# Two PSUM banks that serve sums and filler alike, two open value segments, filled strips, a split root and new exp prices in a two-layer transformer kernel

## The chip, the cores and the metric

The kernel runs on one core of one Trainium2 chip. The metric is device time in microseconds. TensorE is called PE in the profile, VectorE DVE, ScalarE ACT, GpSimdE POOL, SyncE SP; PEld is TensorE's loading of weights.

## The reference

Two identical layers over x (2048 rows of 512): attention with 32 heads of 16 columns, then a dense block with 1792 hidden columns, each behind a layer norm and added to x.

```python
def _layernorm(x, axis=-1, eps=1e-5):
    m = jnp.mean(x, axis=axis, keepdims=True)
    v = jnp.var(x, axis=axis, keepdims=True)
    return (x - m) / jnp.sqrt(v + eps)
...
        scores = jnp.einsum("bhqd,bhkd->bhqk", q, k) * (Dh ** -0.5)
        p = _softmax(scores, axis=-1)
        o = jnp.einsum("bhqk,bhkd->bhqd", p, v)
...
        h = jnp.einsum("bsd,df->bsf", x, w1)
        h = jnp.maximum(h, zero)
        return jnp.einsum("bsf,fd->bsd", h, w2)
...
    x = x + _A_ref(_layernorm(x, axis=-1), A_wqkv, A_wo)
    x = x + _B_ref(_layernorm(x, axis=-1), B_w1, B_w2)
    x = x + _A_ref(_layernorm(x, axis=-1), A_wqkv, A_wo)
    x = x + _B_ref(_layernorm(x, axis=-1), B_w1, B_w2)
```

Everything comes in and goes out as bf16.

## The kernel before, in words

**The slots.** Scores are computed transposed, 128 keys by up to 512 queries of one head: a unit. The loop at L1566 walks all units of both layers, three to a slot (W = 3). In a slot, three score matmuls (L1714), each on 32 rows of the array, write three PSUM banks of ps_s; there are two such sets, used in turn. Then one exp on ScalarE (L1727) reads them and writes bf16 into one of five buffers e. The exp is either wide (all three units) or narrow (two units). In a narrow slot VectorE takes the third unit: its first step (L1299) turns the scores into int16 numbers in a buffer lin, and when two such blocks are there (a pair), GpSimd makes two shifted copies, up and down (L1354). The three together stand for the exp when each is multiplied with the values. There are six lin, three up and four down buffers. A slot is made narrow only if the conditions at L1590 to L1619 hold; one of them, lin_free, asks that the lin buffer six pairs back has been read by its value matmuls and copied by GpSimd.

**The value matmuls.** pv (L1171) multiplies an e, lin, up or down block with the values of one head, into 32 of the 128 partitions of the sums. Four heads fill the four strips of a round (v_round, L1213); the four matmuls of a round run side by side. A segment is one set of four heads, every second of eight, over a range of key blocks. Its sums collect in the bank ps_o. When no matmul of a segment remains, finish_segment (L1026) has VectorE copy the sums out (L1060, L1035 or L1058), and the next segment starts in ps_o after that copy. Only the current segment's blocks are looked at (v_ready with segs[seg_at[0]]).

**The filler.** All other matrix work (q, k, v, output projection, both dense matmuls, transposes of the normed rows) is cut into groups whose pieces stand in `urgent`, `work` and `cur`. A piece is a round of four matmuls on 32 columns each (L564). A group's sums collect in ps_f, and VectorE takes them out (for instance L874, L745, L781, L835, L914) before the next group starts there. Only in the very first slots, while `two[0]` holds, does filler use both banks.

**The planner.** The order on every engine is made when the program is built. Python code keeps a clock per engine (now_pe, now_dve, now_pool, exp_end) with prices: 216 ns for a round, 105 for a switch between kinds of matmul, 612 for an evacuation, and for an exp

```python
        exp_end[no] = begin + 1280.0 * place[m] / (W * QS) + 63.3
```

(L1735; place[m] is 1024 or 1536). For each slot it computes `limit`, the time until which TensorE may do other work without making the exp late (L1689), and fills that time with filler and value rounds (L1691 to L1695): first all filler that is owed, then values in rounds of at least three strips, then filler, or values first when four exps are pending. `owed` grows by `pace` per slot, the filler left over the slots left (L1673). If five exps are pending, force_v (L1259) makes value rounds at once. Where spare time is left, score matmuls are repeated.

**VectorE's order.** run_dve (L468) takes the evacuations of sums and the first steps (`musts`) ahead of filler evacuations, those ahead of tasks. A task is one entry however many instructions it has. The inverse root of a layer norm is one task (L673, ln_root at L616): per chunk of four row blocks four aggregations, two instructions for a first guess, four for a cubic step and three for a Newton step. It is priced RSTD = 1600 ns and is put at the head of the queue (place=0). Behind it come the normed rows (L636), and behind those the transposes, for some chunks by DMA on SyncE (L683).

**The tail.** After the loop the last values, projection, norm and dense block of the last 128 rows run by a written order (L1768 on).

## Time and profile before

| what | us |
|---|---|
| median of 3 runs (1453.84 to 1458.4) | 1454.89 |
| profiled execution | 1457.04 |
| its span, first to last instruction | 1455.3 |
| busy in it: ACT | 1388.2 |
| busy in it: PE | 1367.2 |
| busy in it: DVE | 1137.0 |
| busy in it: POOL | 711.3 |

A group's row names line, engine, operation, output and inputs with their shapes and the count; behind the first bar stand busy time in us and the mean length of one instruction in ns, behind the second the engine's idle time just before these instructions and what ended it. A row of the timeline begins with start and length in us, and merges neighbours of one kind. A row of the windows has the stretch, its length, each engine's busy time and count, TensorE's granted clock, the share of DMA time and GB/s. A row of waits names who waited for whom: us in total, times, the longest.

### The profile page before, as it was taken

How to read it: one execution, taken by the hardware profiler on the slowest of the kernel's cores; microseconds unless marked ns; L12 is line 12 of the kernel's file. 1: busy time of each engine (PE TensorE's matmuls, PEld its weight loads, DVE VectorE, ACT ScalarE, POOL GpSimd, SP SyncE). 2: the span in 40 equal slices, each digit the busy share in tenths (PEclk: the TensorE clock that was granted, in tenths of full speed). 3: DMA queues.
4: the chain of work that ended last, by engine and by line, in shares of the span. 5: the costliest groups of instructions: out<-in, count | busy, mean ns of one | idle time of the engine just before them, and what ended most of it. 6: DMA issues, size and time to landing. Idle time of an engine off the chain costs nothing.

```text
span 1455.3 us, 49098 instructions
## 1 busy us (share of the span) xinstructions
PE 1367.2 (94%) x20895; PEld 497.9 (34%) x20898; DVE 1137.0 (78%) x2078; ACT 1388.2 (95%) x1392; POOL 711.3 (49%) x1203
## 2 busy tenths in 40 slices
PE   6899889999999999999899999989999999999997
PEld 2322222222232222222222222223234444455665
DVE  5777668877887888887698777788888787877773
ACT  4999999999999999999999998999999999999994
POOL 3125555655545555565346453444544555555430
PEclk8999999999899999999999999999999999999999
DMA  5300000210102110121101100000110111132121
GB/s 131 96 5 17 21 21 2 46 39 17 24 8 47 28 31 10 29 49 25 23 2 31 34 5 2 6 18 17 42 42 16 43 37 25 30 83 66 26 49 31
DMA packets 135036, 46.41 MB, mean 32 GB/s; under 512 B 119680, under 2 KB 132032, under 8 KB 134816
## 3 DMA queue, kind: packets, MB, share of 16 engines
q1 hardware_dynamic: 127760, 37.14, 10.9%
q0 software_dynamic: 5568, 5.15, 1.9%
q8 instruction: 163, 2.67, 0.8%
q10 hardware_dynamic: 1488, 0.98, 0.2%
q14 instruction: 57, 0.47, 0.1%
HBM read 24.38 MB, written 2.10 MB: 18 GB/s over the span
## 4 chain that ended last, share of the span: by engine, by line
ACT 50%; PE 35%; DVE 12%; issue 3%; POOL 0%; DMA 0%; DVEq 0%; another core or an unknown queue 0%; ACTq 0%; POOLq 0%
ACT e L1727 50%; PE ps_s L1714 12%; PE ps_o L1175 11%; PE ps_f L564 10%; DVE lin L1299 5%; DVE stats L600 1%; PE ps_s L1801 1%; DVE vaug L781 1%; DVE ht L874 1%; PE ps_f L645 1%; DVE xn L636 0%; PE ps_f L557 0%; DVE ya L611 0%; DVE x L914 0%; DVE u L1060 0%
## 5 line engine op out<-in xcount | busy, mean ns | idle before, releaser
L1727 ACT ACTIVATE e<-ps_s 128x1024 bf16<-128x1024 f32 (+1 forms) x1366 | 1377.3, 1148 | 30.3 <-PE ps_s L1714 25.4
L1299 DVE TENSOR_SCALAR lin<-ps_s 128x512 int16<-128x512 f32 x1106 | 743.8, 686 | 179.8 <-PE ps_s L1714 124.9
L1354 POOL INT64_ADD up<-lin x553 | 340.0, 619 | 587.4 <-PE ps_o L1175 305.0
L1714 PE MATMUL ps_s<-q,ktp 32*128 32x512 bf16 (+2 forms) x5971 | 574.2, 328 | 45.2 <-ACT e L1727 27.6
L1354 POOL INT64_ADD down<-lin x553 | 342.2, 621 | 106.6 <-DVE lin L1299 50.4
L1175 PE MATMUL ps_o<-e,vaug 128*32 128x512 bf16 (+2 forms) x4124 | 365.2, 330 | 8.0 <-DVE r L1060 2.8
L1714 PEld LDWEIGHTS <-ktp 32*128 32x128 bf16 x5971 | 169.6, 91 | 513.5 <-issue 500.9
L1175 PEld LDWEIGHTS <-vaug 128*32 128x32 bf16 x7256 | 169.2, 95 | 228.7 <-issue 203.3
L1175 PE MATMUL ps_o<-up,vaug 128*32 128x512 bf16 (+2 forms) x1508 | 177.8, 324 | 0.0
L1175 PE MATMUL ps_o<-lin,vaug 128*32 128x512 bf16 (+2 forms) x1508 | 169.6, 324 | 1.6 <-DVE u L1060 1.0
L1175 PE MATMUL ps_o<-down,vscaled 128*32 128x512 bf16 (+2 forms) x1392 | 170.8, 326 | 0.0
L564 PE MATMUL ps_f<-xnT,w 128*32 128x512 bf16 (+1 forms) x1792 | 124.2, 356 | 4.6 <-DVE ht L874 2.1
L564 PE MATMUL ps_f<-w,ht 128*32 128x512 bf16 x1680 | 127.0, 382 | 1.3 <-DVE ht L874 0.5
L564 PE MATMUL ps_f<-xnT,wkq 128*32 128x512 bf16 (+2 forms) x1376 | 97.6, 357 | 3.9 <-DVE vaug L781 1.5
L874 DVE TENSOR_SCALAR ht<-ps_f 128x512 bf16<-128x512 f32 x105 | 71.7, 683 | 18.8 <-PE ps_f L564 16.9
L1175 PEld LDWEIGHTS <-vscaled 128*32 128x32 bf16 x1392 | 58.3, 96 | 20.6 <-issue 8.9
L564 PEld LDWEIGHTS <-w 128*32 128x32 bf16 x1792 | 38.8, 95 | 45.8 <-issue 36.8
L564 PEld LDWEIGHTS <-ht 128*32 128x32 bf16 x1680 | 34.7, 95 | 42.2 <-issue 29.1
L564 PEld LDWEIGHTS <-wkq 128*32 128x32 bf16 x1376 | 31.2, 96 | 39.2 <-issue 29.7
L600 DVE BATCH_NORM_STATS2 stats<-x 128x6 f32<-128x512 bf16 x63 | 42.4, 684 | 0.4
L564 PE MATMUL ps_f<-wv,xnT 128*32 128x512 bf16 x496 | 39.0, 383 | 3.8 <-DVE vaug L781 2.2
L564 PE MATMUL ps_f<-wo,ot 128*32 128x512 bf16 x496 | 38.4, 383 | 0.8 <-DVE x L835 0.5
(143 smaller groups left out, 537.4 us busy)
## 6 DMA issues: line engine op xcount, KB each, us to landing
w<-in_B_w_dram SPq DMA_DIRECT2D x144, 128.0 KB
q<-xn SPq DMA_DIRECT2D x44, 64.0 KB
out_dram<-x SPq DMA_DIRECT2D x15, 128.0 KB
x<-in_A_x_dram SPq DMA_DIRECT2D x14, 128.0 KB
ktp<-in_B_w_dram SPq DMA_DIRECT2D x10, 128.0 KB
r<-u POOLq DMA_DIRECT2D x8, 128.0 KB, 4.5
u<-u POOLq DMA_DIRECT2D x8, 128.0 KB, 4.6
u<-r POOLq DMA_DIRECT2D x6, 128.0 KB, 4.4
```

What stands on the lines that cost most here:

```text
L564: nc.tensor.matmul(out[cols], lhsT[:, cols], rhs, start=i % k == 0, stop=i % k == k - 1, tile_position=(0, 32 * g), skip_group_check=True,)
L600: nc.vector.bn_stats(out=stats[ln_n(tag)][:, i, :], in_=x_t[tt][:])
L645: ins = nc.tensor.transpose(pt[:, c * P : (c + 1) * P], xnbuf[i][:, c * P : (c + 1) * P], ident[:])
L781: nc.vector.tensor_copy(out=v_out(l, kb), in_=v_in(b))
L874: nc.vector.tensor_scalar(out=out, in0=sums, scalar1=0.0, scalar2=None, op0=ALU.max)
L1175: nc.tensor.matmul(ps_o[32 * g : 32 * g + 32, 0 : sg["w"]], values[:, 4 * sg["T"] + g, 2 * e : 2 * e + 32], rhs, start=g not in sg["begun" ...
L1299: first = nc.vector.tensor_scalar(out=lin[which][:, half * QS : (half + 1) * QS], in0=src, scalar1=EXP_BIAS, scalar2=THIRD, op0=ALU.add, o ...
L1354: nc.gpsimd.int64_add(words(out), words(line), by)
L1714: score = nc.tensor.matmul(b[:, a : a + sg["w"]], kt[32 * g : 32 * g + 32, kc : kc + P], qbuf[sg["n"] % 2][32 * g : 32 * g + 32, sg["e"], ...
L1727: ex = nc.scalar.activation(out=eb[:, 0 : place[m]], in_=b[:, 0 : place[m]], func=ACTF.Exp, scale=1.0 / (LOG2E * UNIT),)
L1801: uses(nc.tensor.matmul(out, lhsT, rhs, start=first, stop=last), b, needs=needs)
```

## The change

- **Banks.** ps_o and ps_f each have an owner: a segment, filler, or nobody. A segment takes the free bank that came free first when its first round is made; a filler group does likewise, and leaves a bank for a current segment that has none. While all value work is over (`ending`) filler has ps_f.
- **Second segment.** When the current segment has at most 14 units still to come (NEAR), nothing is urgent, pace is at most 1.6 (EASY), no filler is due within 14 slots and the widths agree, the next segment may open in the other bank, except for the last ones (FIXED). If three strips of it are ready and it has no bank, no new filler group starts (HOLD). A value round is filled from the current segment first and from the next one where a strip has nothing.
- **Strips.** A strip that a value round leaves empty is given to the filler group under way, one column at a time (grid_column); a group keeps a count per strip. This holds for groups of whole 512-column rounds.
- **Order in a slot.** One piece at a time: a filler piece if owed, a value round with four strips, one with three, then filler up to eight units ahead of what is owed. Values come first with four exps pending, or when a segment has at most six matmuls left.
- **Root.** Four tasks, at the end of the queue, priced 155 ns per row block, 700, 780 and 580. The instructions are the same.
- **Exps.** Priced 50.0 ns above the streaming time in place of 63.3.
- One GpSimd addition of a small tile, whose result is not used, after the loop.

The core of the diff:

```diff
-        if not two[0] or any(e[3] == 1 for e in evac):
+        if ending[0]:
             return 0
-        if any(e[3] == 0 for e in evac):
-            return 1
-        return int(bank_free[1] < bank_free[0])
+        free = [n for n in range(2) if owner[n] is None]
+        sg = segs[seg_at[0]] if seg_at[0] < len(segs) else None
+        if not two[0] and not forced and sg is not None and sg["bank"] is None:
+            taken = seg_bank(sg)
+            free = [n for n in free if n != taken and taken is not None]
+        return min(free, key=lambda n: bank_free[n]) if free else None
...
+    def grid_column(g):
+
+        G = grid[0]
+        if G is None or not G["cols"][g] or G["ready"] > now_pe[0] - MM:
+            return
+        grid_cell(G["cols"][g].popleft(), g)
+        owed[0] -= 0.25
+        grid_settle()
...
-            task(
-                RSTD, lambda: ln_root(tag, n), [("rs", tag, 3)], each(n, "st", tag) + old, place=0
-            )
+            made_last = each(n, "st", tag) + old
+            for k, step in enumerate(ln_steps(tag, n)):
+                task((155 * n, 700, 780, 580)[k], step, [("rs", tag, k)], made_last)
+                made_last = [("rs", tag, k)]
...
         nc.tensor.matmul(
-            ps_o[32 * g : 32 * g + 32, 0 : sg["w"]],
+            (ps_f, ps_o)[sg["bank"]][32 * g : 32 * g + 32, 0 : sg["w"]],
...
+    def next_seg():
+
+        at_next = seg_at[0] + 1
+        if two[0] or at_next >= len(segs) - FIXED:
+            return None
+        sg, after_it = segs[seg_at[0]], segs[at_next]
+        if sg["bank"] is None or sg["w"] != after_it["w"]:
+            return None
+        if after_it["bank"] is None and (
+            sg["left"] > NEAR or urgent or pace > EASY
+            or any(due.get(g["makes"][0], 1e9) < slot[0] + SPARE_SLOTS for g in work)
+        ):
+            return None
+        return after_it
...
+        after_it = next_seg()
+        if after_it is not None and seg_bank(after_it) is not None and v_start(after_it) <= t:
+            of_it = v_ready(after_it, t)
+            heads_now = {f[1][2] for f in found}
+            found += [f for f in of_it if f[1][2] not in heads_now]
...
+        for g in range(4):
+            if not any(f[1][2] == g for f in found):
+                grid_column(g)
...
-        for kind in ("v", "f", "v") if late else ("f", "v", "f"):
-            if kind == "f":
-                fill_pe(limit)
-            else:
-                fill_v(limit, LEAST.get(no, 3))
...
+            while True:
+                closing = seg_at[0] < len(segs) and sum(segs[seg_at[0]]["rem"]) <= CLOSING
+                late = closing or len(pend) >= PRESSED
+                steps = [
+                    lambda: fill_pe(limit, most=1), lambda: fill_v(limit, 1 if closing else 4, 1)
+                ]
+                steps = (steps[::-1] if late else steps) + [
+                    lambda: fill_v(limit, 3, 1), lambda: fill_pe(limit, -AHEAD_BY, 1)
+                ]
+                if not any(step() for step in steps):
+                    break
...
-        exp_end[no] = begin + 1280.0 * place[m] / (W * QS) + 63.3
+        exp_end[no] = begin + 1280.0 * place[m] / (W * QS) + 50.0
...
+    nc.gpsimd.tensor_add(out=half_va[0][:], in0=half_ya[0][:], in1=half_ya[0][:])
```

More of the change, by code (lines that the diff above doesn't have):

```diff
@@ L574, in mm_group @@
             pieces.append((min(per, n - a) * wide_by / QS, piece))
-        return group(pieces, makes, deps, "t" if whole else "f")
+        in_cells = per == 1 and sums == 1 and wide_by == QS and not whole
+        return group(
+            pieces, makes, deps, "t" if whole else "f",
+            {"mms": mms, "fin": fin, "cost": cost, "after": after} if in_cells else None,
+        )
     chunks = {(l, j): (j * TPC, TPC) for l in range(2) for j in range(NQS)}
@@ L1215, in v_round @@
         pe_run("v", 1, t)
-        sg = segs[seg_at[0]]
-        for n in range(QS // sg["w"]):
+        for sg in {id(f[1][0]): f[1][0] for f in found}.values():
+            if sg["bank"] is None:
+                sg["bank"] = seg_bank(sg)
+                owner[sg["bank"]] = sg
+        for n in range(QS // found[0][1][0]["w"]):
             for g in range(4):
```

202 lines of the change are left out of this document (139 added, 63 removed).

## The prediction

> **What bounds the kernel now.** I read the page first: shares of the engines, then the groups with their shapes kept apart.
>
> ```profile
> span 1455.3 us, 49098 instructions
> ...
> PE 1367.2 (94%) x20895; PEld 497.9 (34%) x20898; DVE 1137.0 (78%) x2078; ACT 1388.2 (95%) x1392; POOL 711.3 (49%) x1203
> ```
> ```profile
> L1727 ACT ACTIVATE e<-ps_s 128x1024 bf16<-128x1024 f32 x1106 | 1040.8, 1067 | 22.7 <-PE ps_s L1714 20.0 <-PE ps_o L1175 0.7 <-ACT e L1727 0.2
> L1299 DVE TENSOR_SCALAR lin<-ps_s 128x512 int16<-128x512 f32 x1106 | 743.8, 686 | 179.8 <-PE ps_s L1714 124.9 <-POOL down L1354 26.7 <-ACT e L1727 5.3
> L1727 ACT ACTIVATE e<-ps_s 128x1536 bf16<-128x1536 f32 x259 | 366.1, 1496 | 7.6 <-PE ps_s L1714 5.4 <-PE ps_o L1175 1.4
> ```
>
> ScalarE does almost nothing but exps, one per slot of three units of scores. A narrow exp (128x1024) means that VectorE and GpSimd took the third unit; a wide one (128x1536) means that ScalarE kept all three. The second number behind the bar is the length of one instruction, not the step from one to the next, since neighbours overlap. So I measured the step in stretches of one kind (start, length of the stretch, count), with the length of the last instruction beside it.
>
> ```profile
> 544.88 9.28 ACT L1727 ACTIVATE e<-ps_s 128x1024 bf16<-128x1024 f32 x10
> ```
> ```profile
> L1727 ACT ACTIVATE e<-ps_s x2: 1138/1145/1152, 552.1 to 553.0; 128x1024 bf16<-128x1024 f32 x2
> ```
> ```profile
> 280.02 17.57 ACT L1727 ACTIVATE e<-ps_s 128x1024 bf16<-128x1024 f32 x19
> ```
> ```profile
> 40.83 9.52 ACT L1727 ACTIVATE e<-ps_s 128x1536 bf16<-128x1536 f32 x7
> ```
>
> At its best a narrow step is (9.28 - 1.145) / 9 = 0.904 us. In an ordinary stretch with no visible idle it is (17.57 - 1.07) / 18 = 0.917. A wide step is (9.52 - 1.50) / 6 = 1.337. A wide slot therefore costs 0.42 us more than a narrow one.
>
> ```profile
> 22.00:1430.00 1408.00, 1377.33 (x1366) 0.99 0.13 30
> ```
>
> That window holds the whole loop of exps. At best steps it would be 1106 x 0.904 + 259 x 1.337 = 1346 us, and it is 1408: 62 us are waits, though the idle columns show only 30, because a wait under about 0.15 us hides under the overlap. So two sums can shrink: 62 us of waits, and 259 x 0.42 = 109 us of wide slots.
>
> **The split root.** The first place to look is where the clock column falls below 1. Eight windows, ScalarE's exps alone (window, us, busy, count, clock):
>
> ```profile
> 238.00:258.00 20.00, 17.42 (x19) 0.83 0.03 8
> ...
> 365.00:384.00 19.00, 15.44 (x17) 0.73 0.16 33
> ...
> 532.00:545.00 13.00, 11.65 (x12) 1.00 0.22 42
> ...
> 582.00:592.00 10.00, 8.98 (x10) 1.00 0.00 0
> ...
> 703.00:715.00 12.00, 10.28 (x11) 0.86 0.23 45
> ...
> 880.00:890.00 10.00, 6.68 (x7) 0.66 0.00 0
> ...
> 1189.00:1203.00 14.00, 12.89 (x14) 1.00 0.18 37
> ...
> 1273.00:1289.00 16.00, 14.51 (x15) 1.00 0.43 92
> ```
>
> Window minus busy adds up to 2.58 + 3.56 + 1.35 + 1.02 + 1.72 + 3.32 + 1.11 + 1.49 = 16.2 us, over half of all visible idle, in 8% of the loop. The timeline of the first shows one cause:
>
> ```profile
> 239.88 0.15 DVE L606 BATCH_NORM_AGGREGATE mv<-stats 128x2 f32<-128x6 f32 x1
> ...
> 242.36 0.16 DVE L628 SCALAR_TENSOR_TENSOR ya<-ta,ya 128x4 f32<-128x4 f32 x1
> 242.47 0.69 DVE L1299 TENSOR_SCALAR lin<-ps_s 128x512 int16<-128x512 f32 x1
> ...
> 243.22 0.37 PE L1714 MATMUL ps_s<-q,ktp 32*128 32x512 bf16 x1 [1.64 <-DVE lin L1299]
> ...
> 244.49 1.94 ACT L1727 ACTIVATE e<-ps_s 128x1024 bf16<-128x1024 f32 x2 [1.16 <-PE ps_s L1714]
> ```
>
> The root (L606 to L628) runs as one task on VectorE. Behind it stands the first step (L1299), which frees the score bank; behind that the score matmuls; behind them the exp. The planner prices the root at 1.6 us, but the row of its last instruction ends 2.64 us after the one quoted first. TensorE's 1.64 us gap is followed by the half clock. The change cuts the root into four tasks priced 0.62, 0.70, 0.78 and 0.58; urgent first steps are chosen ahead of any task, so they stand behind at most one piece, some 0.8 us, and the planner now knows of the full 2.68. The instructions are the same. The rest of the norm, and the transposing DMAs on SyncE or transposes on TensorE behind it, come later by the first steps that slip between, some 0.7 us each; that is hidden as long as the next chunk's keys are not due at once. Ends: 0 if the pieces run together anyway, 25 if the hidden waits behind the clock drops go too. I take **-18**.
>
> The Trainium skill ("TensorE: Matmul & The Clock Gate", Part 1) lets the clock fall after an idle window of about 3.4 us. Here 1.64 us of gap, with thin work around it, already goes with a mean clock of 0.83: the trace sets the nearer limit. By the page alone only the 1.16 us stall itself would be saved at this place.
>
> **The second segment.** Wide exps are not spread evenly.
>
> ```profile
> L1727 ACT ACTIVATE e<-ps_s 128x1536 bf16<-128x1536 f32 x44 | 61.4, 1498 | 2.1 <-PE ps_s L1714 2.1
> ```
> ```profile
> L1727 ACT ACTIVATE e<-ps_s 128x1024 bf16<-128x1024 f32 x442 | 414.0, 1078 | 9.1 <-PE ps_s L1714 8.4
> L1727 ACT ACTIVATE e<-ps_s 128x1536 bf16<-128x1536 f32 x64 | 91.3, 1516 | 0.3
> ```
> ```profile
> L1727 ACT ACTIVATE e<-ps_s 128x1536 bf16<-128x1536 f32 x26 | 36.9, 1512 | 0.9 <-PE ps_s L1714 0.9
> ```
>
> These are the windows 22 to 104 (44 wide, the start, where values are not made yet), 167 to 670 (64) and 715 to 845 (26). The rest, 125, lie mostly behind 845. In the middle they come as two or three together every 20 us or so, at segment ends:
>
> ```profile
> 296.30 0.39 PE L1175 MATMUL ps_o<-e,vaug 128*32 128x512 bf16 x1
> ...
> 297.96 0.61 PE L1175 MATMUL ps_o<-e,vaug 128*32 128x512 bf16 x7
> 298.20 0.59 PE L1175 MATMUL ps_o<-lin,vaug 128*32 128x512 bf16 x4
> 298.41 0.59 PE L1175 MATMUL ps_o<-up,vaug 128*32 128x512 bf16 x4
> ```
> ```profile
> 297.12 0.68 DVE L1060 COPY u<-ps_o 128x512 f32<-128x512 f32 x1
> ```
> ```profile
> POOL up L1354 <- PE ps_o L1175: 305.0, 145, 6.3
> ```
>
> At 296.30 a lone value matmul fills one strip of four and ends a segment; VectorE copies the sums out (297.12 to 297.80), and no value matmul starts until 297.96, when five rounds of the next segment come at once. Until then the pairs of the next segment keep their lin, up and down buffers, GpSimd waits (305 us in 145 waits), and the planner, which asks for a free lin buffer before it starts a pair, leaves the slot wide. With a second segment open in the other bank these values can go earlier. It opens only near a segment's end and where filler is thin (pace up to 1.6 rounds per slot):
>
> ```profile
> 167.00:670.00 503.00, 142.73 (x1816) 0.98 0.12 26
> ...
> 715.00:845.00 130.00, 43.71 (x576) 1.00 0.09 21
> ```
>
> L564's matmuls are a quarter of a round each: 454 rounds over 442 + 64 slots is 0.9, and 144 over some 128 is 1.1. So it can open in just these two windows, with 90 wide slots. Ends: 0, if filler nearly always holds the other bank, and 90 x 0.42 = 38. I take 40 slots, **-17**. Each converted slot costs VectorE 0.686 us (27 us in all, against 318 idle) and TensorE two more strips, half a round of 0.21 (298.41 - 298.20): 4 us, in rounds that are to be filled anyway.
>
> **Repriced exps.** The planner's price of a narrow exp falls from 916.6 to 903.3 ns, of a wide one from 1343.3 to 1330. The trace has 0.904 at best, and 0.917 in the ordinary stretch: what the planner believed, TensorE was packed to. Over 1365 slots 13.3 ns are 18 us. Ends: -18 if all of it was real delay; +18 if the same 18 us of matmuls (some 85 rounds) then stand in the way elsewhere. The ordinary row is nearest to the first: **-10**.
>
> **Filled strips, either bank, order of rounds.** Filler columns in empty strips save part rounds. That lies on TensorE beside a bound ScalarE, so only few waits go: 0 to -8, taken as **-2**. A piece at a time, with filler up to eight units early, moves evacuations forward on a VectorE that is idle 22%; musts still go first, and weight loads on SyncE follow their group. I cost it at nothing; if that cover is gone, filler is late next (below).
>
> ```profile
> 1430.00:1456.00 26.00, 17.75 (x248) 12.86 (x239) 8.28 (x28) 6.22 (x18) 0.00 (x0) 1.00 0.05 16
> ```
>
> The added GpSimd sum after the loop lies beside a tail where GpSimd does nothing for 26 us: nothing.
>
> **Sum.** The profiled execution took 1457.0 us (span 1455.3): 1457 - 18 - 17 - 10 - 2 = 1410. It lay 2.1 above the median of the runs, 1454.9, so the forecast for the median is **1408**.
>
> **Rivals.** *Only the small prices pay.* Filler owns the other bank at nearly every boundary and the second segment does not open. For it: TensorE is 94% busy. Against: filler is told to start no group when three strips wait. 1455 - 18 - 10 = 1427, or 1437 without the repricing.
>
> *All of it pays:* 38 + 25 + 18 = 81, so 1374.
>
> *Filler held off.* While both banks hold sums no filler can start; it comes back later in one lump, scores wait behind it, ScalarE behind them. The price stands in this row, where filler rounds already ran four and five deep between scores:
>
> ```profile
> 685.00:703.00 18.00, 16.54 (x18) 1.00 0.10 21
> ```
>
> 1.46 us per such place. It decides from 47 / 1.46 = 32 places on. At two to three wide slots each, the 215 wide slots after the start make some 86 boundaries; a lump at half of them is 63 us, so 1455 - 47 + 63 = 1471, slower. Against it: the second segment needs thin filler and nothing due soon.
>
> The Trainium skill (same page, "A second HAM failure mode: psum-queue depth-cycling") tells of kernels that swap PSUM banks and let the clock swing. It would come out here as more stretches like 880 to 890, where 10 us held 6.68 of exps; 15 more, at 3.3 us, would eat the gain and give about 1457. The clock of 1.00 in most windows, with filler and sums in two banks already, speaks against it; I keep 0.05 for it.
>
> **Chances.** Forecast (1395 to 1425) 0.50; only the small prices 0.20; all of it (below 1395) 0.12; filler held off 0.13; the swinging clock, within 0.3% of before, 0.05. Three tenths of a per cent is about what can be told from no change here. Faster 0.82, same 0.05, slower 0.13. The range, 1382 to 1452, takes in the forecast, the first rival and most of the second.
>
> **What would show it.** Root right: no window of exps with a clock below 1 after 100 us, and L1299 rows between those of L611 to L628. Second segment right: clearly fewer than 259 wide exps, lost between 167 and 845, and shorter GpSimd waits on L1175. Repricing right: ordinary narrow steps near 0.905. Filler held off: long filler blocks and exp idle at deadlines. Wrong altogether if wide exps rise, or if L1714 becomes the end of more ScalarE idle than 25 us.

## The result, and the profile after

The changed kernel takes 1442.72 us (median of 4 runs, 1440.34 to 1443.88), the kernel before 1454.37 beside it: a ratio of 0.991, 95% interval 0.989 to 0.992. It is faster by 11.7 us where 47 were forecast. The profiled execution took 1440.34 us, 16.7 less than the one of before.

The page of the kernel after (busy time, share of the span, instructions), and its groups of exps and first steps:

```profile
span 1438.6 us, 48761 instructions
...
PE 1360.0 (95%) x20779; PEld 496.8 (35%) x20781; DVE 1132.1 (79%) x2066; ACT 1387.9 (96%) x1394; POOL 702.1 (49%) x1192
```
```profile
L1868 ACT ACTIVATE e<-ps_s 128x1024 bf16<-128x1024 f32 x1094 | 1026.9, 1121 | 16.1 <-PE ps_s L1855 8.5 <-PE ps_o L1250 3.8 <-PE ps_f L1250 1.8
L1868 ACT ACTIVATE e<-ps_s 128x1536 bf16<-128x1536 f32 x271 | 383.8, 1539 | 3.5 <-PE ps_s L1855 1.9 <-PE ps_o L1250 1.2
```

Idle time in front of the exps fell from 30 to 20 us, but the wide exps rose from 259 to 271. The second number behind the bar, the mean length of a narrow exp, rose from 1067 to 1121 ns, though the loop got shorter: it is no cost. That is the first thing to put right, for the prediction's base rests on it. Its stretch of ten exps starts at 544.88 and ends 9.28 us later. This row of the kernel before has the first exp of that stretch and the one ahead of it:

```profile
L1727 ACT ACTIVATE e<-ps_s x2: 1018/1025/1032, 544.0 to 544.9; 128x1024 bf16<-128x1024 f32 x2
```

That first exp is 1.032 us long and ends at 545.91. From end to end the nine steps take (554.16 - 545.91) / 9 = 0.917 us; from start to start, as the prediction measured, 0.904, because every exp here is 13 ns longer than the last while the next ones start earlier beside it. (The 0.917 that the prediction gave for an ordinary stretch came by luck: it took the mean length of 1.07 for the last one's 1.125; by its own method it would have been 0.914.) The same in the kernel after, one stretch of the timeline, and its first exp with the one ahead:

```profile
249.31 51.49 ACT L1868 ACTIVATE e<-ps_s 128x1024 bf16<-128x1024 f32 x56
```
```profile
L1868 ACT ACTIVATE e<-ps_s x2: 1059/1066/1072, 248.4 to 249.3; 128x1024 bf16<-128x1024 f32 x2
```

(300.80 - 250.385) / 55 = 0.917. Over all records the median step between the ends of two narrow exps is 0.917 us in both kernels, and no step is under 0.912; between wide ones it is 1.343. So 0.917 and 1.343 are what ScalarE takes, and what lies above them is waits: 44.3 us in the kernel before, where the prediction counted 62. With these two steps every kernel's time splits into four parts: when the first exp starts, the number of wide exps (0.426 us more than a narrow one), the waits in the loop, and the tail from the last exp's end to the end of the last computing instruction. The parts are those of each kernel's profiled execution; the last column says how far that one lies above or below the median:

| kernel | median us | ratio to before, 95% | first exp | wide | waits | tail | profiled - median |
|---|---|---|---|---|---|---|---|
| before | 1454.4 | 1 | 22.3 | 259 | 44.3 | 22.5 | +2.7 |
| **after** | 1442.7 | 0.991 (0.989 to 0.992) | 12.1 | 271 | 26.7 | 28.5 | -2.4 |
| before + GpSimd sum | 1445.1 | 0.993 (0.991 to 0.995) | 12.2 | 259 | 41.2 | 22.5 | -1.4 |
| before + split root | 1462.8 | 1.005 (1.003 to 1.007) | 21.5 | 257 | 36.4 | 38.0 | 0.0 |
| the same, pieces at the head | 1457.5 | 1.002 (1.001 to 1.004) | 21.9 | 267 | 31.3 | 34.5 | +1.2 |
| before + price 50 | 1463.0 | 1.005 (1.003 to 1.007) | 21.6 | 259 | 35.1 | 36.5 | -2.2 |
| after, no GpSimd sum | 1449.3 | 0.996 (0.995 to 0.997) | 23.3 | 271 | 31.0 | 28.5 | +6.5 |
| after, 64-bit sum last | 1449.5 | 0.996 (0.994 to 0.997) | 22.2 | 271 | 25.6 | 28.4 | -0.2 |
| after, root in one task | 1446.5 | 0.994 (0.992 to 0.996) | 12.1 | 263 | 46.6 | 23.4 | +5.0 |
| after, price 63.3 | 1446.9 | 0.994 (0.992 to 0.996) | 12.2 | 257 | 37.6 | 29.0 | -1.1 |
| after, no strips | 1442.1 | 0.990 (0.989 to 0.992) | 12.1 | 277 | 25.6 | 28.5 | -0.4 |
| after, one segment (output off, see below) | 1436.3 | 0.987 (0.985 to 0.989) | 12.1 | 283 | 21.2 | 23.9 | -0.8 |
| after, no hold rule | 1433.1 | 0.984 (0.983 to 0.986) | 12.1 | 263 | 21.6 | 29.7 | +0.3 |
| one segment, no strips | 1430.1 | 0.982 (0.981 to 0.984) | 12.3 | 289 | 14.8 | 24.3 | +1.8 |
| second segment for 8 units, no hold, no strips | 1436.8 | 0.988 (0.986 to 0.991) | 12.2 | 291 | 21.5 | 25.4 | +3.7 |
| one segment, no strips, 63.3 | 1436.7 | 0.988 (0.986 to 0.990) | 12.1 | 267 | 23.7 | 29.7 | +0.1 |
| no hold, NEAR 8, head, 63.3 | 1429.6 | 0.982 (0.980 to 0.983) | 12.1 | 253 | 31.6 | 22.4 | +1.6 |

The last column belongs in the main to the waits: two kernels with the same loop (before with and without the GpSimd sum, after with and without it) agree in wide exps and tail and differ in the waits, by 3.1 and 4.3 us. It goes with TensorE's clock: the 42 executions of the kernel before beside these took 1458.2 us on average where the mean clock was 0.985 (5 of them) and 1452.8 where it was 0.991 (2). So "at the median" below means waits less the last column, an estimate.

The kernel before took 1454.4 to 1455.8 beside these. Medians two to three us apart are not told apart by such runs. The expectations below count waits against the steps of 0.903 and 1.330; their numbers are 19 us above the table's (1365 steps of 13 to 14 ns).

From before to after, in the profiled executions: the start -10.2, the waits -17.6, twelve wide exps more +5.1, the tail +6.0. Together -16.7, which is the whole difference of these two executions. The medians differ by 11.7; with the last column the waits account for some -12.5. The largest part outside the waits is one that the prediction put at nothing.

### The profile page after: what moved, and what is told of

Same layout as the page of the kernel before. It is cut to its first block, busy times and chain, and to the rows that moved or that the text cites. A ratio compares the mean times of both kernels' runs of the same rounds, so it can differ in the third digit from the quotient of the medians.

```text
span 1438.6 us, 48761 instructions
## 1 busy us (share of the span) xinstructions
PE 1360.0 (95%) x20779; PEld 496.8 (35%) x20781; DVE 1132.1 (79%) x2066; ACT 1387.9 (96%) x1394; POOL 702.1 (49%) x1192
## 4 chain that ended last, share of the span: by engine, by line
ACT 24%; PE 23%; DVE 5%; issue 2%; POOL 0%; DMA 0%; DVEq 0%; POOLq 0%; ACTq 0%
ACT e L1868 24%; PE ps_s L1855 7%; PE ps_o L1250 5%; PE ps_f L419 4%; PE ps_f L1250 2%; DVE lin L1427 2%; PE ps_o L419 2%; PE ps_f L624 1%; PE ps_s L1943 1%; DVE ht L949 1%; PE ps_o L624 0%; PE ps_f L617 0%; DVE down L1486 0%; DVE r L1138 0%; DVE u L1138 0%
## 5 line engine op out<-in xcount | busy, mean ns | idle before, releaser
L1427 DVE TENSOR_SCALAR lin<-ps_s 128x512 int16<-128x512 f32 x1094 | 734.4, 686 | 142.7 <-PE ps_s L1855 107.3
L1482 POOL INT64_ADD up<-lin x547 | 336.6, 619 | 583.2 <-DVE lin L1427 294.6
L1482 POOL INT64_ADD down<-lin x547 | 335.8, 617 | 90.0 <-DVE lin L1427 35.2
L1250 PE MATMUL ps_o<-e,vaug 128*32 128x512 bf16 (+2 forms) x2466 | 211.0, 310 | 5.5 <-DVE r L1138 1.4
L1250 PE MATMUL ps_f<-e,vaug 128*32 128x512 bf16 (+2 forms) x1666 | 184.1, 355 | 3.6 <-DVE u L1138 1.4
L1250 PE MATMUL ps_f<-up,vaug 128*32 128x512 bf16 (+2 forms) x638 | 106.2, 350 | 0.0
L1250 PE MATMUL ps_o<-lin,vaug 128*32 128x512 bf16 (+2 forms) x862 | 103.5, 305 | 1.5 <-DVE r L1138 0.6
L1250 PE MATMUL ps_f<-lin,vaug 128*32 128x512 bf16 (+2 forms) x638 | 101.2, 349 | 2.2 <-DVE r L1138 0.7
L1250 PE MATMUL ps_o<-up,vaug 128*32 128x512 bf16 (+2 forms) x862 | 102.9, 305 | 0.3 <-POOL up L1482 0.2
L1250 PE MATMUL ps_f<-down,vscaled 128*32 128x512 bf16 (+2 forms) x582 | 102.7, 352 | 0.0
L1250 PE MATMUL ps_o<-down,vscaled 128*32 128x512 bf16 (+2 forms) x804 | 93.1, 306 | 0.9 <-issue 0.9
L1250 PEld LDWEIGHTS <-vscaled 128*32 128x32 bf16 x1386 | 59.5, 96 | 28.5 <-issue 22.0
L419 PE MATMUL ps_o<-w,ht 128*32 128x512 bf16 x840 | 65.1, 381 | 2.1 <-DVE x L989 1.8
L419 PE MATMUL ps_f<-w,ht 128*32 128x512 bf16 x784 | 64.7, 382 | 0.2 <-DVE vaug L1114 0.2
L419 PE MATMUL ps_o<-xnT,w 128*32 128x512 bf16 x688 | 57.8, 382 | 1.1 <-DVE ht L949 0.6
L419 PE MATMUL ps_f<-xnT,w 128*32 128x512 bf16 x656 | 54.4, 382 | 1.6 <-DVE ht L949 0.6
L419 PEld LDWEIGHTS <-ht 128*32 128x32 bf16 x1680 | 40.9, 96 | 35.5 <-issue 20.8
L419 PE MATMUL ps_f<-xnT,wkq 128*32 128x512 bf16 x560 | 46.4, 382 | 2.8 <-DVE vaug L1114 0.8
```

Of the source, the lines that this page charges most:

```text
L419: nc.tensor.matmul(G["b"][cols], lhsT[:, cols], rhs, start=not G["begun"][g], stop=not G["cols"][g], tile_position=(0, 32 * g), skip_group ...
L1250: nc.tensor.matmul((ps_f, ps_o)[sg["bank"]][32 * g : 32 * g + 32, 0 : sg["w"]], values[:, 4 * sg["T"] + g, 2 * e : 2 * e + 32], rhs, start ...
L1427: first = nc.vector.tensor_scalar(out=lin[which][:, half * QS : (half + 1) * QS], in0=src, scalar1=EXP_BIAS, scalar2=THIRD, op0=ALU.add, o ...
L1482: nc.gpsimd.int64_add(words(out), words(line), by)
```

## The experiments

**The GpSimd sum.** The timeline of GpSimd at the start, before and after (start, length; in brackets what it waited for):

```profile
0.81 0.20 POOL masks.py:197 MEMSET ident<- 128x128 bf16 x1
9.52 0.28 POOL masks.py:199 TENSOR_SCALAR_AFFINE_SELECT ident<-ident 128x128 bf16<-128x128 bf16 x1 [8.50 <-issue]
```
```profile
0.81 0.20 POOL masks.py:197 MEMSET ident<- 128x128 bf16 x1
1.30 0.29 POOL masks.py:199 TENSOR_SCALAR_AFFINE_SELECT ident<-ident 128x128 bf16<-128x128 bf16 x1 [0.29 <-POOL ident masks.py:197]
```

Before, GpSimd waits 8.50 us for nothing that the profile shows ("issue") between a memset and the instruction that finishes the identity matrix; VectorE waits for that matrix (8.71 us) before it starts the first norm, and the transposes of the head come behind the norm. After, the wait is gone, and the first exp starts 10 us earlier. Two kernels take this one line alone: put into the kernel before, and taken out of the kernel after.

```diff
         do_task(t)
+    nc.gpsimd.tensor_add(out=half_va[0][:], in0=half_ya[0][:], in1=half_ya[0][:])
     users.clear()
```

> The kernel before with nothing but the unused GpSimd addition after the loop. The profile of the changed kernel starts its exps 10 us earlier, and the 8.5 us that GpSimd stood still ahead of the identity at the very start are gone there. Theory: the addition at the end puts GpSimd back to its ordinary code, so that the next execution does not begin with fetching it; then this kernel alone is 8 to 10 us faster than before, all of it ahead of the first exp, with the loop unchanged (259 wide exps, waits of some 60 us). Rival: the early start comes from something else in the changed program, and this kernel is within 2 us of before.

> The changed kernel without the GpSimd addition after the loop. Theory: 8 to 10 us slower than the changed kernel, all ahead of the first exp, so that the rest of the change is worth only some 2 to 6 us against before. Rival: as fast as the changed kernel.

Measured: 1445.1 (-9.7) and 1449.3 (+6.6). The second is less than the 8 to 10 expected, though its first exp starts 11.2 us later; its profiled execution lies 6.5 above its median. What an instruction at the end can do for the start is seen at the end itself, in the timeline of GpSimd after:

```profile
1404.67 0.61 POOL L1482 INT64_ADD up<-lin  x1 [3.37 <-PE ps_o L1250]
1412.42 0.18 POOL L1923 TENSOR_TENSOR half_va<-half_ya 128x2 f32<-128x2 f32 x1 [7.14 <-issue]
```

But for DMA issues the loop's GpSimd work is 64-bit integer sums (L1482). The first ordinary sum behind them waits 7.14 us for nothing shown, beside a tail in which GpSimd has no other work. The theory: going from the one kind to the other costs that much; the kernel before ends on the first kind, and its next execution pays at the start. The test adds one more 64-bit sum at the very end.

```diff
     nc.gpsimd.tensor_add(out=half_va[0][:], in0=half_ya[0][:], in1=half_ya[0][:])
+    nc.gpsimd.int64_add(trial, trial, PACKED)
```

> The changed kernel with one 64-bit integer addition (4 bytes x 2 per partition) on GpSimd behind the added sum after the loop, so that GpSimd ends on the kind of operation that it ends on in the kernel before. Theory (what GpSimd ran last in one execution sets what it waits for at the start of the next): the wait of about 8.5 us before its first row comes back, the first exp starts near 21 to 23 us in place of 12.1, and the time is 1450 to 1453, as without the sum at all (1449.3 in its own run). Rival (the sum helps by being there, or by where it stands in the tail): the first exp stays near 12 us and the time near 1443.

Measured: 1449.5, the first exp at 22.2. The timeline of GpSimd in this kernel, start and end:

```profile
9.46 0.28 POOL masks.py:199 TENSOR_SCALAR_AFFINE_SELECT ident<-ident 128x128 bf16<-128x128 bf16 x1 [8.44 <-issue]
```
```profile
1421.23 0.18 POOL L1923 TENSOR_TENSOR half_va<-half_ya 128x2 f32<-128x2 f32 x1 [6.84 <-PE ps_s L1944]
1427.40 0.18 POOL L1924 INT64_ADD up<-up  x1 [5.98 <-issue]
```

The time is 0.5 under the range expected. The ordinary sum is still there and the wait at the start is back, 8.44 us. So it is the last kind of instruction that counts, not the sum as such. The way back to the 64-bit kind costs 5.98 us too. The Trainium skill ("GPSIMD Engine Reference", section 2.1 Instruction dispatch) tells of about 6 us, with no instruction to show for it, when GpSimd first calls a freshly loaded kernel; the 5.98 agrees with that. That a wait reaches into the next execution is shown by these runs alone.

**The root.** In the kernel after, the root runs in pieces. VectorE's timeline of one of them (L679 aggregates, L682 to L686 first guess, L692 to L695 cubic step, L698 to L700 Newton step):

```profile
397.72 0.37 DVE L679 BATCH_NORM_AGGREGATE mv<-stats 128x2 f32<-128x6 f32 x4
398.22 0.79 DVE L856 CAST vaug<-ps_o 128x512 bf16<-128x512 f32 x1
398.88 1.50 DVE L1427 TENSOR_SCALAR lin<-ps_s 128x512 int16<-128x512 f32 x2
400.30 0.16 DVE L682 TENSOR_SCALAR va<-mv 128x4 f32<-128x4 f32 x1
...
402.92 1.27 DVE L1427 TENSOR_SCALAR lin<-ps_s 128x512 int16<-128x512 f32 x2
404.11 0.28 DVE L692 TENSOR_TENSOR ta<-ya 128x4 f32<-128x4 f32 x1
...
409.86 0.16 DVE L700 SCALAR_TENSOR_TENSOR ya<-ta,ya 128x4 f32<-128x4 f32 x1
```

First steps (L1427) slip between the pieces, and the whole takes 12.3 us where it took 2.6. TensorE's waits for first steps, before and after (total, times, longest):

```profile
PE ps_s L1714 <- DVE lin L1299: 11.8, 12, 1.6
```
```profile
PE ps_s L1855 <- DVE lin L1427: 1.9, 4, 0.7
```

One kernel undoes the split in the kernel after, one does it alone in the kernel before, one does it there with the pieces at the head of the queue.

```diff
-            made_last = each(n, "st", tag) + old
-            for k, step in enumerate(ln_steps(tag, n)):
-                task((155 * n, 700, 780, 580)[k], step, [("rs", tag, k)], made_last)
-                made_last = [("rs", tag, k)]
+            task(
+                1600.0, lambda: ln_root(tag, n), [("rs", tag, 3)], each(n, "st", tag) + old, place=0
+            )
```

> The changed kernel with the root as one task again, at the head of VectorE's queue and priced 1600 ns. Theory of the prediction: the stalls with the clock drops at the roots come back, 15 to 20 us slower than the changed kernel. Theory now: the split alone made the kernel before slower, by what it leaves for the tail; the stalls come back, but less filler is left after the last exp, and this kernel is 0 to 10 us slower.

> The kernel before with the split root and its prices alone. Theory of the prediction: no clock drop after the start, the waits of exps fall by 15 to 25 us, and so does the time. Rival: the pieces let the rest of the norm slip so that other waits take their place, and the gain is under 8 us.

Undone: 1446.5, and the clock drops at the roots are back. Windows around four roots, exps alone (stretch, length, busy and count, granted clock, DMA share, GB/s), first with the root in one task, then the kernel after:

```profile
230.00:250.00 20.00, 16.80 (x18) 0.83 0.03 8
526.00:544.00 18.00, 14.94 (x16) 0.91 0.12 24
759.00:779.00 20.00, 17.93 (x19) 0.83 0.04 8
877.00:895.00 18.00, 15.51 (x13) 0.91 0.03 9
```
```profile
228.00:248.00 20.00, 19.64 (x21) 1.00 0.03 9
518.00:536.00 18.00, 18.00 (x19) 1.00 0.08 16
744.00:764.00 20.00, 20.00 (x22) 1.00 0.03 9
868.00:886.00 18.00, 18.00 (x16) 1.00 0.03 9
```

The waits are 46.6 with one task and 26.7 with four, 20 less. But the profiled execution with one task lies 5.0 above its median (its mean clock is the lowest of four, 0.989 against 0.992 to 0.994) and the one with four tasks 2.4 below: at the median some 12.5 of the 18 us forecast are left. And that the loop of the kernel after shows no fall at all is in part luck: the same loop, profiled without the GpSimd sum, has three (at 161.27, 1018.02 and 1355.94 us), though none at a root. How a drop comes about is in the timeline of TensorE with the root in one task:

```profile
235.90 0.54 PE L1854 MATMUL ps_s<-q,ktp 32*128 32x512 bf16 x1 [1.46 <-DVE lin L1426]
236.37 0.61 PE L1249 MATMUL ps_o<-up,vaug 128*32 128x512 bf16 x1
```

A gap of 1.46 us, and the matmuls behind it take 0.54 to 0.61 us instead of 0.39, for 6.8 us by the clock's record. The Trainium skill ("TensorE: Matmul & The Clock Gate", Part 1) has the clock fall after an idle window of about 3.4 us. Here no gap is that long: the five falls within the loop of this kernel stand behind gaps of 1.46, 1.98, 0.91, 1.51 and (two close together) 0.52 us, so the measurement decides: a wait for one long task can be enough. It need not be: in the same profile gaps of 1.35 us (at 587.6) and 2.52 us (at 692.4) passed without a fall. The kernel before and the same with the GpSimd sum have the same loop. Here is one wait in both; a fall follows at 371.55 in the first, none in the second:

```profile
370.19 0.37 PE L1714 MATMUL ps_s<-q,ktp 32*128 32x512 bf16 x1 [1.63 <-DVE lin L1299]
```
```profile
362.50 0.37 PE L1714 MATMUL ps_s<-q,ktp 32*128 32x512 bf16 x1 [1.63 <-DVE lin L1299]
```

In every trace the changes of the clock lie whole multiples of 3.413 us apart (from 371.55 back to 252.08, for one, 35 of them). Cut at these points, the first kernel has the whole gap in one stretch and the second has it across two. TensorE in these stretches (stretch, length, busy and count, clock):

```profile
368.14:371.55 3.41, 1.78 (x19) 1.00 0.00 0
```
```profile
358.14:361.55 3.41, 2.73 (x32) 1.00 0.00 0
361.55:364.97 3.42, 2.47 (x27) 1.00 0.19 38
```

In the kernel before, the four falls of the loop end its four least busy stretches after the first 40 us (49 to 60%). So where a gap falls on this grid matters beside its length, which fits the spread between executions. No limit can be read off: over all the profiles one stretch of 54% had no fall (one task, ending at 696.8), and one of 74% had one (second segment for 8 units, ending at 917.7).

But the time went down by 4 us only, and the intervals of the two ratios touch: the split came with eight more wide exps (+3.4) and a tail 5.1 longer. On the kernel before, the split alone made it 8 us slower. The windows of TensorE from the end of the last exp on, before and with the split alone:

```profile
1429.80:1452.20 22.40, 17.95 (x263) 1.00 0.04 13
```
```profile
1420.10:1458.10 38.00, 31.16 (x437) 1.00 0.26 64
```

174 more matmuls lie behind the last exp, 13 us of TensorE. The loop is 9 us shorter in these two executions (1398.6 against 1407.4), and what it has not done by its end comes afterwards, where no exp hides it. A second loss lies at the passage between the layers. ScalarE's exps there, slots 650 to 714, before and with the split:

```profile
685.70:756.40 70.70, 66.95 (x67) 0.98 0.08 17
```
```profile
676.80:758.30 81.50, 72.69 (x66) 0.98 0.07 15
```

The last test asks whether the place of the pieces in the queue makes these losses.

```diff
-                task((155 * n, 700, 780, 580)[k], step, [("rs", tag, k)], made_last)
+                task((155 * n, 700, 780, 580)[k], step, [("rs", tag, k)], made_last, place=k)
```

> The kernel before with the split root alone, its four pieces put at the head of VectorE's queue one behind the other instead of at its end. Theory (the place in the queue makes the split alone slow: pieces wait behind filler evacuations, the norm of the next layer slips, and the hand-over near 700 us stalls): the 65 slots from 650 on lose most of their 25 wide exps and 12.2 us of waits (before: 14 and 6.0), and the time is 1452 to 1456, against 1462.8 with the pieces at the end. Rival (the loop shortened by the split leaves its filler to the tail, whatever the place): the tail stays at 33 to 38 us and the time at 1458 to 1464.

Measured: 1457.5, between the two ranges; the tail is 34.5 and the 65 slots keep their 25 wide exps. So the rival holds for the mechanism, if not to the microsecond: whatever the place, the loop leaves work to the tail. The place accounts for some 5 us. What makes the passage between the layers slow in these two kernels is known in part. This row of VectorE stands there with the split alone:

```profile
716.05 0.69 DVE L827 TENSOR_SCALAR xn<-ps_f 128x512 bf16<-128x512 f32 x1 [5.20 <-DMA xnT<-xn]
```

An evacuation into xn waits 5.20 us for the transposing DMA that reads the normed rows there, and TensorE stands still for 2.10 us behind it. With the pieces at the head the wait is 5.3; the kernel before, the one after and the one with the root undone have no such wait. The rest of the loss there stays open.

**The price of an exp.** One line, tried three times: 50.0 in the kernel before, 63.3 in the kernel after, and 63.3 in the kernel with one segment and no strips (below).

```diff
-        exp_end[no] = begin + 1280.0 * place[m] / (W * QS) + 63.3
+        exp_end[no] = begin + 1280.0 * place[m] / (W * QS) + 50.0
```

> The kernel before with the exp prices lowered by 13.3 ns alone. Theory of the prediction: ordinary narrow steps fall from 0.917 to about 0.905 us, 10 us less in all. Rival, since the changed kernel still shows ordinary steps of 0.917: the step has 13 ns of its own scatter whatever the planner believes; then the time is the same within 4 us or, because less work fits a slot in the plan, longer.

> The changed kernel with the old exp prices, 13.3 ns higher. Theory of the prediction: 10 us slower, ordinary narrow steps at 0.917 in place of 0.905. Theory now: those steps are 0.917 in both, and the higher price is the truer one; the plan is then not slower, and the time is within 4 us of the changed kernel or shorter.

> The changed kernel with one segment open at a time, without filled strips and with the old exp price of 63.3. Theory (a longer price leaves room between the score matmuls for value rounds, so fewer slots stay wide, and what the exps wait for is not the price): wide exps 267 in place of 289 (-9), waits a few us up, 1421 to 1427. Rival (the lower price pays as it did in the changed kernel as a whole, where 63.3 cost 4): 1432 to 1438.

The last two came out otherwise than expected: 63.3 cost the kernel after 4.2 us, neither theory's number, and cost the other 6.6, the rival's. In all three pairs the lower price takes waits away: 44.3 to 35.1, 37.6 to 26.7, 23.7 to 14.8, that is -9.2, -10.9 and -8.9 (at the median -4.3, -9.6 and -10.6). And in all three something is given back elsewhere: a tail 14 us longer in the kernel before, 14 more wide exps (+6.0) in the kernel after, 22 more (+9.4, with a tail 5.4 shorter) in the last. The medians move by +8, -4 and -6.6 us. The step stayed at 0.917 in all of them. With 63.3 the planner's narrow exp was 916.6 ns, what the chip takes; with 50.0 its clock runs ahead of the chip by 13.3 ns a slot. Score matmuls then come early, exps start earlier beside one another (hence the mean length of 1121 in place of 1067), and small delays no longer reach ScalarE. That the room for value rounds shrinks by the same amount is the reading that fits the wide exps and the tails; no run measures it. The groups of exps show both, here with one segment and no strips, first at 63.3, then at 50.0:

```profile
L1868 ACT ACTIVATE e<-ps_s 128x1024 bf16<-128x1024 f32 x1098 | 1033.3, 1066 | 8.4 <-PE ps_s L1855 5.2 <-PE ps_o L1250 1.1 <-PE ps_f L1250 0.6
L1868 ACT ACTIVATE e<-ps_s 128x1536 bf16<-128x1536 f32 x267 | 378.3, 1494 | 3.8 <-PE ps_s L1855 2.5 <-PE ps_o L1250 1.1
```
```profile
L1868 ACT ACTIVATE e<-ps_s 128x1024 bf16<-128x1024 f32 x1076 | 1013.5, 1132 | 7.4 <-PE ps_s L1855 5.8 <-PE ps_f L1250 0.7
L1868 ACT ACTIVATE e<-ps_s 128x1536 bf16<-128x1536 f32 x289 | 411.7, 1547 | 2.9 <-PE ps_s L1855 1.5 <-PE ps_o L1250 1.1
```

**The second segment.** GpSimd's waits after (total, times, longest):

```profile
POOL up L1482 <- DVE lin L1427: 294.6, 233, 14.8
POOL up L1482 <- PE ps_f L1250: 125.5, 35, 15.2
POOL up L1482 <- PE ps_o L1250: 107.8, 50, 6.1
```

Its waits for value matmuls fell, from 305 us to 125.5 + 107.8 = 233, as forecast; but it waits more for first steps (253.9 before), and its idle time as a whole is nearly what it was (744 us before, 736 after). Where the wide exps lie tells why. Two neighbouring stretches of 66 exps, one of them in both (shortest, median and longest in ns, first and last start, shapes):

```profile
L1868 ACT ACTIVATE e<-ps_s x66: 1018/1154/1538, 742.4 to 803.2; 128x1024 bf16<-128x1024 f32 x63, 128x1536 bf16<-128x1536 f32 x3
```
```profile
L1868 ACT ACTIVATE e<-ps_s x66: 1023/1218/1652, 803.2 to 875.7; 128x1024 bf16<-128x1024 f32 x37, 128x1536 bf16<-128x1536 f32 x29
```

Three are wide in the first and 29 in the second. The filler matmuls (L419) of the kernel after in the same two stretches:

```profile
743.00:804.00 61.00, 11.82 (x145) 3.29 (x145) 1.00 0.07 17
804.00:876.00 72.00, 33.48 (x416) 9.80 (x416) 1.00 0.10 24
```

Filler is held off in the first, 36 rounds, and comes back in the second, 104. While it does, value rounds have less room (345 value matmuls in the first stretch, 272 in the second), and, as we read it, pairs stay unread longer. Kernels that take the parts away follow: no second segment; no hold rule; no strips; no strips and no second segment; and no strips and no hold rule, with the second segment for 8 units.

```diff
-        if two[0] or at_next >= len(segs) - FIXED:
+        if True or two[0] or at_next >= len(segs) - FIXED:
```

> The changed kernel with only one segment open at a time; everything else of it stays. Theory now: the second segment does what the prediction said at the boundaries, where wide exps were many, but the filler that it holds off comes back in the second half of each chunk with wide exps of its own; so without it wide exps move to the boundaries, the count rises by little from 271, and the time is within 6 us of the changed kernel, on either side. Theory of the prediction: without it some 40 wide exps come back and 17 us are lost.

What this kernel puts out is off by a relative error of 0.12, for a reason that is not known, so its time is no more than a hint; its count of matmuls is within 0.4% of the kernel after, and the same edit without strips, below, has no such fault. Measured: 1436.3. There are 12 more wide exps, 283, but the waits are 5.5 and the tail 4.6 less.

```diff
-    NEAR, HOLD, SPARE_SLOTS, EASY, FIXED = 14, 3, 14, 1.6, 3
+    NEAR, HOLD, SPARE_SLOTS, EASY, FIXED = 14, 9, 14, 1.6, 3
```

> The changed kernel without the rule that keeps new filler groups from starting when three strips of the next segment wait for a bank. Theory: that rule is what delays filler; without it fewer wide exps stand in the second halves of the chunks (slots 455 to 520, 585 to 715, 780 to 845 held 20, 36 and 26), and the time falls by 5 to 10 us. Rival: filler then holds the second bank at every boundary, the wide exps at the boundaries come back, and the time is the same within 4 us or longer.

Measured: 1433.1, 9.6 less than the kernel after. Its filler matmuls in the same 130 slots (715 to 844), halved:

```profile
735.00:800.00 65.00, 20.06 (x240) 5.53 (x240) 1.00 0.12 28
800.00:865.00 65.00, 26.60 (x304) 7.35 (x304) 1.00 0.05 12
```

Each half now has 12 wide exps; there were 3 and 25 in the same slots. The lump is gone.

```diff
-        if G is None or not G["cols"][g] or G["ready"] > now_pe[0] - MM:
+        if True or G is None or not G["cols"][g] or G["ready"] > now_pe[0] - MM:
```

> The changed kernel without filler columns in the empty strips of value rounds; all else as it is. Theory (the strips save part rounds on TensorE, which lies beside a bound ScalarE): 2 to 5 us longer, 1445 to 1448; the planner itself plans 278 wide exps in place of 272 (6 x 0.43 = 2.6). Rival (the columns delay value rounds and hold a filler group's bank for longer): shorter, 1435 to 1440.

> The changed kernel with one value segment open at a time and without filled strips, to be read against the run without filled strips alone. Theory (the second segment keeps filler out of the bank, and the filler that comes back late costs more than the boundary saves): 4 to 8 us shorter than without filled strips alone, although the planner plans more wide exps (290 against 278, which by itself would be +5), since waits between exps fall by some 10. Rival (as the forecast had it, the second segment saves 40 wide slots): 5 to 17 longer.

Without strips 1442.1: neither theory's number, the strips do nothing that can be told in the kernel after. Without strips and with one segment 1430.1, 12 less, and more than expected: 12 more wide exps (+5.1), but waits down by 10.8 and the tail by 4.2. It is also 6.2 less than one segment with strips (1436.3; the intervals of the two ratios do not meet): there the strips cost time, by longer waits (21.2 against 14.8), with the reserve that the 1436.3 is the kernel whose output is off. So what a part is worth hangs on which others are in.

> The changed kernel without the hold rule (HOLD 9), the second segment opening only for the last 8 units, and without filled strips; to be read against one segment without filled strips (1430.1). Theory (only the hold rule costs; the second segment by itself neither saves nor costs): 1428 to 1434. Rival (a second open segment costs by itself, since it takes the bank that filler had): waits between exps of 40 or more in place of 33.7, and 1436 to 1442.

Measured: 1436.8, with waits of 21.5 against 14.8 and two more wide exps: the rival. So the hold rule is the larger part, but a second segment without it gains nothing either: 6.7 slower here, 3 faster with strips and 14 units (1433.1 against 1436.3, not clearly told apart).

**A version put together.** No hold rule, the second segment for the last 8 units only, the root's pieces at the head of the queue, 63.3.

> The changed kernel without the hold rule (HOLD 9), the second segment opening only for the last 8 units (NEAR 8), the four pieces of the root at the head of VectorE's queue, and the old exp price (63.3). Theory (the filler held off, and the filler and norms handed on to the tail, are what the change loses): wide exps 254 in place of 271 (-7), waits between exps as without the hold rule or a little above for the old price (40 to 50), tail 23 to 25 in place of 28.5: 1424 to 1430. Rival (each edit of the rules only draws another plan, and plans scatter by 5 to 10): no better than without the hold rule alone, 1433 to 1442.

Measured: 1429.6. The tail is 22.4 and the wide exps are 253, the fewest, as expected; the waits, 31.6, are 10 above those without the hold rule. The rival is not ruled out: 1429.6 and the 1433.1 without the hold rule are 3.5 apart, and the intervals of their ratios overlap. It and the kernel with one segment and no strips (1430.1) are the fastest, 0.982 of before and some 13 us under the kernel after, and they get there on opposite sides: 253 wide exps and 31.6 of waits, or 289 and 14.8.

## Why the prediction went wrong, step by step

- **The sum as a whole.** It was -47 and the time moved by -11.7, within the range and with the sign right. Part of that is luck: without the GpSimd sum, which was put at nothing, the kernel takes 1449.3, so the terms that were to bring 47 brought 5.5. Each term was taken at the place where it acts, and nothing was put in for where TensorE's work goes. TensorE is busy 94% before and 95% after. What is saved at one place (waits) is filler or value rounds that have to be done at another: as wide exps or as a longer tail. In all six pairs of the table in which the price or the split takes waits away, the wide exps or the tail rise. Six pairs make this likely, not certain: each edit draws another plan of the whole, and by how much plans scatter without any cause was not measured.
- **The GpSimd sum, "nothing".** The step that failed reads only the tail, where the sum is indeed hidden. What it does lies at the start of the next execution: -9.7 alone, -6.6 in the kernel after. The row was there to be seen, 8.50 us of GpSimd waiting for nothing shown, at the start of the profile of before.
- **The split root, -18.** The mechanism was right: no fall of the clock at a root, first steps between the pieces. Its size in the waits was 20 in the profiled executions (46.6 to 26.7), some 12.5 at the median. The step that failed is "that is hidden as long as the next chunk's keys are not due at once": what is late next is the work that a shorter loop has not done by its end (a tail 5.1 longer in the kernel after, 15.5 alone), and, with the split alone, an evacuation that waits 5.20 us for the transposes at the passage between the layers. The net is about -4 in the kernel after and +8 alone.
- **The second segment, -17.** The step that failed is "I take 40 slots". It makes 12 wide exps fewer (283 to 271, and 289 to 277), 20 without the hold rule (283 to 263), which is -5 to -8.5; and with the hold rule it costs 5 to 11 us of waits (7 to 13 at the median) and some 5 in the tail: net +6 to +12. Without the rule the net lies between -3 and +7. The rival "filler held off" named this mechanism and priced it at 63 us; with the hold rule it measured 10. The sentence that filler is told to start no group when three strips wait stood as a reason for the gain; that rule is the cost.
- **Repricing, -10.** The size was right in the waits of the last two pairs (-9.6 and -10.6 at the median; -4.3 in the kernel before) and the reason wrong. The ordinary step did not fall from 0.917, since that is ScalarE's own; the 0.904 was a difference of starts. "What the planner believed, TensorE was packed to" held for TensorE alone: it was packed 13.3 ns a slot tighter than the chip's exps need, which covers small delays and crowds out value rounds. The net is -4 here, +8 alone.
- **Strips, -2.** Nothing measurable in the kernel after (1442.1 without, 1442.7 with). With one segment they cost some 6 us (1436.3 with, 1430.1 without).
- **Order of rounds, filler eight units ahead, "nothing".** Not tried by themselves.
- **What would show it.** The clock came as written in the profiled execution, in part by luck (above); the first steps between the root's pieces and the shorter waits of GpSimd came too. The swinging clock of the last rival did not come. The rise of the wide exps was named as the sign that the forecast is wrong altogether, and it is the sign that came.

## What to carry to other kernels

Where the second engine is busy for 94% beside a bound one, a rule that moves its work is to be priced by where that work lands, not by the wait that goes: split the time into start, unavoidable steps, waits and tail, and look at all four. Measure a step between ends, over instructions that overlap, and treat a mean length that grows as no cost. And read the first microseconds of every engine: a wait for nothing shown, at the start, may be set by the last instruction of the program.

## What the runs showed of the hardware

- GpSimd needed 6 to 9 us between a 64-bit integer sum and an ordinary instruction: 7.14 (after, at the end), 5.98 (the other way), 8.50 and 8.44 at the start of an execution that follows one ending on the 64-bit kind. The memsets that stand ahead of it at the start (0.30 to 0.81 us) went without the wait.
- Exps in a row on ScalarE end 0.917 us apart at 1024 columns and 1.343 at 1536, in every kernel here. The length that the profile shows for one grows by 13 ns from each to the next as long as they start 0.903 us (narrow) or 1.330 us (wide) apart.
- TensorE's clock fell to one half for 3.4 to 10.2 us in the loops, each time at a point of a grid of 3.413 us and behind a stretch in which TensorE was busy for 74% or less; the longest gap just before was 0.3 to 2.2 us. Not every such stretch or gap had a fall: 1.63 us had one in one execution and none in another of the same loop. In the kernel after, whose longest wait for a first step is 0.7 us, it stayed at 1.00 from the first exp to the end of the profiled execution.
